# Windowed attention and a gated feed-forward: the gate's low part through PSUM, offsets for the first chunks, and the weights' checks placed by a count

## The chip, the cores and the metric

The kernel runs on one core of one Trainium2 chip. The metric is the device time of one execution in microseconds (us), taken as the median of several runs. TensorE (PE) multiplies matrices and writes to PSUM; VectorE (DVE), ScalarE (ACT) and GpSimd (POOL) work element by element, and POOL works on SBUF alone in this kernel; SyncE (SP) issues the DMAs. Each engine has one queue and runs it in order: an instruction that waits holds up everything behind it on its engine.

## The reference

Two layers, one after the other, in float32. The first is attention over 4 batches, 8 heads, 768 positions of 64 elements, where a position sees the 4 first positions (sinks) and the last 128. The second takes the attention's output as 3072 tokens of 512 elements.

```python
scores = q @ k.T / sqrt(64)                       # per batch and head
keep = (pos_k < 4) | ((0 <= rel) & (rel < 128))   # rel = pos_q - pos_k
a = softmax(where(keep, scores, -1e9))
x = (a @ v) as 3072 x 512
h = x @ w_in                                      # 512 x 2048
g = h * cos(h)
out = g @ w_out                                   # 2048 x 512
```

## The kernel before

**High and low parts.** Matrix products run in a rounded float32 format (fp32r). To keep precision, each operand is held as a rounded high part and a low part, the rest: `hi = round(a)`, `lo = a - hi`. A product is three matmuls, hi by hi, lo by hi and hi by lo. ACT makes the high part by a copy, and DVE or POOL the low part by a subtraction.

**Tiling.** The tokens are cut into 12 chunks of 256. Chunks 0, 1 and 2 are the first 256 positions of batches 0, 1 and 2; their 24 heads are "early": their scores and values are plain float32 matmuls (L737, L925), and the x of their chunks is split by a trick on PE. `x_minus` (L327) adds to the values in PSUM the product of minus the identity and the high part, so that the low part is left there to be copied out (L370, L372). Minus the identity lies in the tile `minus`, which is the first half of `gt`, a buffer that is used later for the sinks.

Each chunk has 8 slots; a slot is 256 of the 2048 hidden columns. There are 96 slots, numbered m = 8a + s for chunk a and slot s. A slot goes through these steps:

- `h_mm` (L381): 24 matmuls of 128 x 256 into a bank of PSUM, the h bank. Chunks 0 and 1 turn over two banks (b4, b2), later ones over three (b4, b2, b3).
- `turns` (L390, ACT) and `rest` (L396, DVE): h in whole turns, and the fraction r that is left of it, in SBUF.
- `cosine` (L403, ACT): r becomes the cosine, by a table of sines. A softmax on ACT needs the table of exponentials, so a change of tables lies between.
- `gate` (L408, DVE): h in PSUM times the cosine, written over r in SBUF. With it the h bank is free.
- `g_hi` (L414, ACT) and `g_lo` (L420, DVE or POOL): the gate's high and low part.
- `out_mm` (L429): 12 matmuls of 128 x 512 into two accumulators, banks b0 and b1. After 8 slots they are copied out (L370, L372) into the tiles `raw` and stored.

**Attention, head by head.** SP loads q, k, v; q and k are turned (L713 by PE for early heads, L695 and L766 by DVE for the others) and split (L778, L784); PE makes scores (L737, L793), DVE masks them (L806), ACT takes the exponential (L815). For four or two heads together DVE makes the denominators (L824, L825), after which every head's p is normalised on POOL, DVE or ACT (L835), transposed by PE (L895), split (L904, L911) or copied, and multiplied by v (L949). The sinks' columns go by a way of their own (L867, L877).

**Weights.** Where the weights come as 64-bit pairs (the case here), 32 pieces of 128 x 512 pairs are loaded into two `raw` tiles and converted. Each piece is loaded once more later, to be checked: `check_piece` has SP load the piece and DVE reduce it to one number per partition (L533), in the column of `tiny`. At the end one number of all of `tiny` decides whether a general path must run again. A check takes a turn of the two `raw` tiles, which the accumulators' copies use too. From chunk 2 on, a slot has one check until all 32 are placed.

**What sets the order.** Nothing reorders the code at run time. The class `Plan` collects every step with the engines that could do it, their durations as estimates, the steps and buffers that it waits for, and a priority: the slot's time t, plus a constant of the step's kind from the table `C`. It then goes through time with a list of ready steps for each engine and always takes the one with the lowest priority; where several engines could do it, by further constants. `emit` writes the steps out in that order. So the constants move each step in the engines' queues, and a changed step moves those around it.

## Time and profile before

| | us |
|---|---|
| runs | 771.24, 774.18, 778.17 |
| median | 774.18 |
| profiled execution, its own time | 773.9 |
| its span | 772.1 |
| mean granted TensorE clock | 0.993 |
| PE busy | 748.2 (97%) |
| weight loads of PE busy | 660.9 (86%) |
| DVE busy | 608.5 (79%) |
| ACT busy | 577.9 (75%) |
| POOL busy | 150.5 (19%) |

The span is the time from the first to the last recorded instruction; the execution's own time holds a little more, 1.8 us here. The engine with the most work is PE. Of its chain of waits, "PE h L381" holds 31% and "PE acc L429" 29% of the span. A share over the whole span hides the stages: the first 120 us, in which weights and the first heads arrive; the middle, in which attention of later chunks runs beside the slots of earlier ones; and the end, in which only slots are left. The views by stretches below keep them apart.

### The profile page before, as it was taken

Reading aid. Unit: us, or ns where it says so; the run is one execution under the profiler, and the core shown is the slowest. Engines: PE = TensorE matmul, PEld = TensorE weight load, DVE = VectorE, ACT = ScalarE, POOL = GpSimd, SP = SyncE. Lnnn points to the kernel's source line nnn. Section 1 sums busy time; section 2 is a strip of 40 time slices with the busy share of each in tenths; the row PEclk is TensorE's granted clock in tenths of the full one; section 3 lists DMA queues with packets and bytes.
Section 4 is the critical chain, followed back from the end, with each engine's and each line's share of the span. In section 5 each row is a group of like instructions: output and inputs, shape, how many; then the busy total and the mean of one; then the engine's idle time right before and its main releaser. Section 6 shows DMA issues by size and latency. Waiting matters only on the chain.

```text
span 772.1 us, 15308 instructions
## 1 busy us (share of the span) xinstructions
PE 748.2 (97%) x4987; PEld 660.9 (86%) x4987; DVE 608.5 (79%) x1597; ACT 577.9 (75%) x1345; POOL 150.5 (19%) x233
## 2 busy tenths in 40 slices
PE   7899999999989999999999999999999999999996
PEld 6566777888978989888899999999999999999995
DVE  6868888778868889989989988888878988964432
ACT  2779796878868787787787887897798788784332
POOL 2122210100313432212234321210211221220000
PEclk9999999999999999999999999999999999999998
DMA  5655464332455366275367243232242233110000
GB/s 149 173 158 170 133 192 156 65 57 39 88 157 110 56 185 163 40 191 138 65 164 187 45 114 54 46 70 45 38 87 53 46 76 60 31 39 1 28 1 32
DMA packets 215673, 71.50 MB, mean 93 GB/s; under 512 B 204320, under 2 KB 204320, under 8 KB 215584
## 3 DMA queue, kind: packets, MB, share of 16 engines
q1 hardware_dynamic: 215584, 70.43, 38.2%
q8 instruction: 41, 0.67, 0.4%
q14 instruction: 48, 0.39, 0.2%
HBM read 64.10 MB, written 6.29 MB: 91 GB/s over the span
## 4 chain that ended last, share of the span: by engine, by line
PE 80%; DVE 7%; DMA 5%; ACT 4%; issue 2%; SPq 1%; DVEq 0%; ACTq 0%
PE h L381 31%; PE acc L429 29%; PE av L949 5%; PE tp L895 4%; PE s L793 4%; DMA raw<-in_moe_w_in_dram 3%; PE s L737 2%; PE av L925 2%; DMA xk<-in_k_dram 1%; ACT p L815 1%; PE gp L877 1%; DVE p L806 1%; DVE plo L911 1%; DVE r L396 1%; SPq L675 1%
## 5 line engine op out<-in xcount | busy, mean ns | idle before, releaser
L381 PE MATMUL h<-xhi,whi_in 128*128 128x256 f32 x768 | 224.0, 292 | 2.4 <-DVE r L408 2.4
L381 PE MATMUL h<-xlo,whi_in 128*128 128x256 f32 x768 | 217.2, 283 | 0.1
L381 PE MATMUL h<-xhi,wlo_in 128*128 128x256 f32 x768 | 216.9, 282 | 0.0
L381 PEld LDWEIGHTS h<-xhi,whi_in 128*128 128x128 f32 x768 | 145.8, 190 | 15.3 <-issue 4.5
L429 PE MATMUL acc<-whi_out,ghi 128*128 128x512 f32 x384 | 157.5, 410 | 0.0
L381 PEld LDWEIGHTS h<-xhi,wlo_in 128*128 128x128 f32 x768 | 146.1, 190 | 7.5
L429 PE MATMUL acc<-wlo_out,ghi 128*128 128x512 f32 x384 | 151.7, 395 | 0.0
L429 PE MATMUL acc<-whi_out,glo 128*128 128x512 f32 x384 | 150.5, 392 | 0.0
L381 PEld LDWEIGHTS h<-xlo,whi_in 128*128 128x128 f32 x768 | 145.8, 190 | 0.3 <-DVE xlo L337 0.3
L806 DVE CUSTOM_DVE_ANT_0 p<-s,mk 128x264 f32<-128x264 f32 (+1 forms) x192 | 76.8, 400 | 33.2 <-PE s L793 21.8
L815 ACT ACTIVATE p<-p,st 128x264 f32<-128x264 f32 (+1 forms) x192 | 93.4, 489 | 0.7
L403 ACT ACTIVATE r<-r,neg 128x512 f32<-128x512 f32 x96 | 69.0, 723 | 26.7 <-DVE r L396 24.3
L429 PEld LDWEIGHTS acc<-whi_out,glo 128*128 128x128 f32 x384 | 72.2, 188 | 16.5
L420 DVE TENSOR_TENSOR glo<-r,ghi 128x512 fp32r<-128x512 f32 x82 | 57.7, 703 | 31.3 <-ACT ghi L414 30.5
L414 ACT CAST ghi<-r 128x512 fp32r<-128x512 f32 x96 | 59.0, 615 | 30.0 <-PE acc L429 29.0
L429 PEld LDWEIGHTS acc<-whi_out,ghi 128*128 128x128 f32 x384 | 72.6, 189 | 5.0 <-issue 0.7
L429 PEld LDWEIGHTS acc<-wlo_out,ghi 128*128 128x128 f32 x384 | 73.0, 190 | 3.8 <-DVE wlo_out L518 0.3
L408 DVE TENSOR_TENSOR r<-h,r 128x512 f32<-128x512 f32 x96 | 65.2, 680 | 11.7 <-ACT r L403 11.4
L390 ACT ACTIVATE yt<-h 128x512 int32<-128x512 f32 x96 | 57.1, 595 | 18.1 <-PE h L381 16.0
L396 DVE SCALAR_TENSOR_TENSOR r<-h,yt 128x512 f32<-128x512 f32 x96 | 65.6, 683 | 5.4 <-ACT yt L390 4.0
L835 POOL TENSOR_SCALAR p<-p,st 128x264 f32<-128x264 f32 (+2 forms) x65 | 36.7, 576 | 156.3 <-DVE st L825 122.3
L848 POOL TENSOR_TENSOR vr<-v,vr 128x192 fp32r<-128x192 f32 (+1 forms) x59 | 34.9, 591 | 160.6 <-ACT vr L843 143.2
(128 smaller groups left out, 1392.8 us busy)
## 6 DMA issues: line engine op xcount, KB each, us to landing
raw<-in_moe_w_in_dram SPq DMA_DIRECT2D x32, 512.0 KB
raw<-in_moe_w_out_dram SPq DMA_DIRECT2D x32, 512.0 KB
xk<-in_k_dram SPq DMA_DIRECT2D x256, 48.0 KB
out_dram<-raw SPq DMA_DIRECT2D x24, 256.0 KB
v<-in_v_dram SPq DMA_DIRECT2D x64, 96.0 KB
xq<-in_q_dram SPq DMA_DIRECT2D x144, 32.0 KB
v<-in_v_dram SPq DMA_DIRECT2D x32, 64.0 KB
xq<-in_q_dram SPq DMA_DIRECT2D x24, 64.0 KB
```

The source lines that it names most:

```text
L381: nc.tensor.matmul(out=o.h[:, t, :], lhsT=w[:, c, fs], rhs=xx[:, c, :], start=(c == 0 and n == 0), stop=(c == NC - 1 and n == 2),)
L390: nc.scalar.activation(out=yt, in_=o.h, func=AF.Copy, scale=INV2PI, bias=0.25)
L396: nc.vector.scalar_tensor_tensor(out=o.r, in0=o.h, scalar=INV2PI, in1=yt, op0=ALU.mult, op1=ALU.subtract)
L403: nc.scalar.activation(out=o.r, in_=o.r, func=AF.Sin, scale=TWOPI_DOWN, bias=quarter)
L408: nc.vector.tensor_tensor(out=o.r, in0=o.h, in1=o.r, op=ALU.mult)
L414: nc.scalar.copy(out=o.ghi, in_=o.r)
L420: e.tensor_tensor(out=o.glo, in0=o.r, in1=f32(o.ghi), op=ALU.subtract)
L429: nc.tensor.matmul(out=x.acc[j], lhsT=gg[:, t, j * P : (j + 1) * P], rhs=w[:, f, :], start=(f == 0 and n == 0), stop=(f == NFT - 1 and n = ...
L806: nc.vector.tensor_tensor_reduce(out=o.p[:, j, :w], in0=o.s_ps[j][:, :w], in1=masks[min(o.i0 + j, 2)][:, :w], op0=ALU.add, op1=ALU.min, sc ...
L815: nc.scalar.activation(out=o.p[:, j, :w], in_=o.p[:, j, :w], func=AF.Exp, bias=o.lead.st[:, 0, o.nth, j : j + 1], scale=-1.0, accum_out=o. ...
L835: e.tensor_scalar(out=o.p[:, j, :w], in0=o.p[:, j, :w], scalar1=r, scalar2=1.0, op0=ALU.mult, op1=ALU.mult)
L949: nc.tensor.matmul(out=dst, lhsT=lhs, rhs=rhs, start=(n == 0), stop=(n == len(seq) - 1), skip_group_check=True)
```

## The change

- `gate` writes its product back over h in PSUM. `g_hi` reads it there, and `g_lo` subtracts from it there; since POOL isn't given PSUM, `g_lo` runs on DVE alone. r is free after the gate, and the h bank only after the low part has been made.
- In chunks 0 and 1 there is a new way (`GM` is 2): `g_minus` adds minus the identity times the high part to the h bank on PE, one matmul of 128 x 512, and `g_rest` copies what is left out as the low part, on ACT or DVE.
- For this the start and stop marks of `h_mm` stand once for the bank rather than once for each half of it.
- The table `FIRST` gives each kind of step in chunks 0, 1 and 2 an offset of its own, and the weights' pieces a slope.
- The checks are placed so that those still missing are no more than 0.87 for each of the last eight slots and 0.371 for each slot before them.
- The constants of `C` are new.

```diff
+    "ALT": 0.104, "BLF": 0.065, "CK": 15.581, "CR": 0.87, "CS": 0.371, "DA": -3.061, "DH": -1.801, "DM": -0.625,
...
+    "POOLF": 0.622, "POOLPEN": 6.121, "PRE": 4.5, "R": 2, "RAW": 2, "SAME": 0.176, "SEM": 0.204, "SPE": 0.29,
...
+FIRST = {
+    "A": [16.64, 4.98, -6.05], "H": [0.49, 0.51, 5.97], "L": [-3.43, 4.39, -1.69], "M": [5.14, -1.3, 1.47],
...
+    def extra(kind, a):
+        return FIRST[kind][a] if a < 3 else 0.0
...
                     nc.tensor.matmul(
                         out=o.h[:, t, :], lhsT=w[:, c, fs], rhs=xx[:, c, :],
-                        start=(c == 0 and n == 0), stop=(c == NC - 1 and n == 2),
+                        start=(t == 0 and c == 0 and n == 0), stop=(t == FG - 1 and c == NC - 1 and n == 2), skip_group_check=True,
                     )
...
-            nc.vector.tensor_tensor(out=o.r, in0=o.h, in1=o.r, op=ALU.mult)
+            nc.vector.tensor_tensor(out=o.h, in0=o.h, in1=o.r, op=ALU.mult)
...
-            nc.scalar.copy(out=o.ghi, in_=o.r)
+            nc.scalar.copy(out=o.ghi, in_=o.h)
...
-            e.tensor_tensor(out=o.glo, in0=o.r, in1=f32(o.ghi), op=ALU.subtract)
+            e.tensor_tensor(out=o.glo, in0=o.h, in1=f32(o.ghi), op=ALU.subtract)
+        return fn
+
+    def g_minus(o):
+        def fn(e):
+            nc.tensor.matmul(out=o.h, lhsT=minus, rhs=o.ghi, start=False, stop=True, skip_group_check=True)
+        return fn
+
+    def g_rest(o):
+        def fn(e):
+            o.glo = mp.tile([P, FG, NT], F32R, name=f"glo_{o.m}", tag="glo", bufs=C["GLO"])
+            copy(e, o.glo, o.h)
         return fn
...
-            a6 = add(sub(FG * NT), g_lo(o), [a5, blo], t + C["DM"] + 10.8, port=True)
-            br.users += [a5, a6]
+            br.users.append(a4)
+            a5 = add([("ACT", act(FG * NT, False))], g_hi(o), [a4, bhi], tm + 10.2)
+            users = [a0, a2, a4, a5]
+            if plan.minus and a < C["GM"]:
+                m = add([("PE", 0.23)], g_minus(o), [a5], tm + 10.5)
+                bhi.users.append(m)
+                env.minus.users.append(m)
+                c = [("ACT", act(FG * NT, False)), ("DVE", dve(FG * NT))]
+                a6 = add(c, g_rest(o), [m, blo], tm + 10.8)
+                users.append(m)
+            else:
+                a6 = add([("DVE", dve(FG * NT))], g_lo(o), [a5, blo], tm + 10.8)
+            bh.users += users + [a6]
...
-            if a > 1 and len(checked) < len(checks):
+            left = len(slots) - nh
+            while len(checked) < len(checks) - C["CR"] * min(left, NSLOT) - C["CS"] * max(left - NSLOT, 0):
                 checked.append(check_piece(plan, t + C["CK"], len(checked), checks[len(checked)][2]))
```

The order of the steps that comes out, at three places. The rows are instructions as they stand in one engine's queue: line, operation, output, inputs, shape. The number after `h_`, `r_` or `glo_` is the slot; after `p_` or `st_` come batch, block of positions and head. In the changed kernel the lines lie 11 to 32 further down.

PE's queue in chunk 0 before the change, between the last accumulating matmul of slot 0 and the first h of slot 4, which takes the bank of slot 2:

```order
L429 MATMUL acc_0_1_912<-whi_out_91,glo_0_836 128x512
L713 MATMUL qk_2_0_2_954<-ident_79,xq_74 128x128 x2
L713 MATMUL qk_2_0_2_954<-ident_79,xk_75 128x128 x2
L895 MATMUL tp_1_0_4_970<-ident_79,p_1_0_4_672 128x128 x3
L381 MATMUL h_4_984<-xhi_0_405,whi_in_89 128x256
```

And now, with the new matmul for slot 2 (L436) ahead of the h of slot 4:

```order
L770 MATMUL s_2_0_3_1_1056<-tk_2_0_2_984,tq_2_0_2_977 128x256
L436 MATMUL h_2_854<-ghi_2_1046,gt_80 128x512
L928 MATMUL tp_1_0_7_1065<-ident_79,p_1_0_7_814 128x128 x3
L338 MATMUL av_1_0_6_1049<-xhi_1_760,gt_80 64x256
L392 MATMUL h_4_1076<-xhi_0_413,whi_in_89 128x256
```

Before, the bank of slot 2 was free when its gate had run; now four short matmuls stand between the minus and the h that takes the bank over, and the copy of the low part has to run beside them.

DVE's queue in chunk 2 before, where the second of two checks stands ahead of a softmax's denominators and normalisations:

```order
L533 ISA wt1_73,tiny_87<-raw1_71 128x512
L533 ISA tiny_87 128x1
L824 TENSOR_SCALAR st_0_2_4_1987<-st_0_2_4_1987 128x8
L825 RECIPROCAL st_0_2_4_1987<-st_0_2_4_1987 128x8
L835 TENSOR_SCALAR p_0_2_4_1986<-p_0_2_4_1986,st_0_2_4_1987 128x264 x2
L835 TENSOR_SCALAR p_0_2_5_2150<-p_0_2_5_2150,st_0_2_4_1987 128x264
L408 TENSOR_TENSOR r_20_2554<-h_20_2467,r_20_2554 128x512
```

And a place in chunk 4 now, one of five of this kind:

```order
L555 ISA wt1_73,tiny_87<-raw1_71 128x512
L555 ISA tiny_87 128x1
L857 TENSOR_SCALAR st_1_2_4_3761<-st_1_2_4_3761 128x8
L858 RECIPROCAL st_1_2_4_3761<-st_1_2_4_3761 128x8
L799 STREAM_TRANSPOSE tk_1_4_2_4297<-xk_75 128x3x128
L419 TENSOR_TENSOR h_35_4126<-h_35_4126,r_35_4208 128x512
L407 SCALAR_TENSOR_TENSOR r_36_4318<-h_36_4217,yt_81 128x512
L898 CAST gc_186<-p_1_2_4_3760 128x2x8
```

The checks stand ahead of the denominators at both; the normalisations have left DVE's queue, for POOL's and ACT's. Over the whole kernel DVE has 75 of the 192 normalisations before and none after, POOL 65 and 133, ACT 52 and 59.

DVE's queue in the last chunk before:

```order
L396 SCALAR_TENSOR_TENSOR r_92_9818<-h_92_9756,yt_81 128x512
L408 TENSOR_TENSOR r_92_9818<-h_92_9756,r_92_9818 128x512
L420 TENSOR_TENSOR glo_91_9859<-r_91_9771,ghi_91_9849 128x512
L396 SCALAR_TENSOR_TENSOR r_93_9864<-h_93_9805,yt_81 128x512
L408 TENSOR_TENSOR r_93_9864<-h_93_9805,r_93_9864 128x512
```

And now:

```order
L555 ISA wt0_72,tiny_87<-raw0_70 128x512
L555 ISA tiny_87 128x1
L431 TENSOR_TENSOR glo_91_9859<-h_91_9718,ghi_91_9852 128x512
L407 SCALAR_TENSOR_TENSOR r_93_9879<-h_93_9821,yt_81 128x512
L555 ISA wt1_73,tiny_87<-raw1_71 128x512
```

Seven checks have moved here, and the low part reads the h bank. Of the other checks, about three stand in each chunk from the third to the eleventh. The low part of chunks 0 and 1 is a copy, eleven times on ACT and five times on DVE, and POOL, which made fourteen low parts before, makes none.

More of the change, by code (lines that the diff above doesn't have):

```diff
@@ L54, in __init__ @@
         self.steps, self.bufs, self.port, self.ahead = [], {}, set(), set()
+        self.minus = False
     def buf(self, tag, n):
@@ L562, in dense @@
                     mm.append(
-                        add([("PE", 0.655)], h_mm(o, x, tt, half), d + mm[-1:], t + C["DH"] + (3.5, 5.8)[tt] + 0.6 * half)
+                        add([("PE", 0.655)], h_mm(o, x, tt, half), d + mm[-1:], t + C["DH"] + extra("H", a) + (3.5, 5.8)[tt] + 0.6 * half)
                     )
@@ L566, in dense @@
             x.blo.users += mm
-            a0 = add([("ACT", act(FG * NT, False))], turns(o), mm + [by], t + C["DM"] + 7.2)
-            a2 = add([("DVE", dve(FG * NT))], rest(o), [a0, br], t + C["DM"] + 8.0)
+            tm = t + C["DM"] + extra("M", a)
+            a0 = add([("ACT", act(FG * NT, False))], turns(o), mm + [by], tm + 7.2)
+            a2 = add([("DVE", dve(FG * NT))], rest(o), [a0, br], tm + 8.0)
             by.users.append(a2)
-            a3 = add([("ACT", act(FG * NT) + 0.09)], cosine(o), [a2], t + C["DM"] + 8.9, table="sin")
-            a4 = add([("DVE", dve(FG * NT))], gate(o), [a3], t + C["DM"] + 9.5)
-            bh.users += [a0, a2, a4]
-            a5 = add([("ACT", act(FG * NT))], g_hi(o), [a4, bhi], t + C["DM"] + 10.2)
-            a6 = add(sub(FG * NT), g_lo(o), [a5, blo], t + C["DM"] + 10.8, port=True)
-            br.users += [a5, a6]
+            a3 = add([("ACT", act(FG * NT) + 0.09)], cosine(o), [a2], tm + 8.9, table="sin")
+            a4 = add([("DVE", dve(FG * NT))], gate(o), [a3], tm + 9.5)
+            br.users.append(a4)
[11 more added lines that the diff above has]
+            bh.users += users + [a6]
             for tt in range(FG):
@@ L603, in banded_path @@
         plan = Plan()
+        plan.minus = True
         add, buf = plan.add, plan.buf
@@ L1052, in before_softmax @@
                     oo.bl = buf("l", C["L"])
-                    q1 = add([("ACT", act(NT))], q_hi(o, oo), [q0, oo.bl], t - 6 * T + C["DQ"] + 0.6)
-                    oo.ql = add([("DVE", dve(NT))], q_lo(o, oo), [q1], t - 6 * T + C["DQ"] + 0.9, port=True)
+                    q1 = add([("ACT", act(NT))], q_hi(o, oo), [q0, oo.bl], t - 6 * T + dq + 0.6)
+                    oo.ql = add([("DVE", dve(NT))], q_lo(o, oo), [q1], t - 6 * T + dq + 0.9, port=True)
                     btq.users += [q1, oo.ql]
@@ L1142, in after_softmax @@
             bav = buf("av", 1)
-            p0 = add([("PE", 0.107 * o.n)], turn(o), o.nm + [pt], t + C["DA"] + 1.3)
+            p0 = add([("PE", 0.107 * o.n)], turn(o), o.nm + [pt], t + da + 1.3)
             o.bp.users.append(p0)
-            p1 = add([("ACT", act(o.n * P, False))], p_hi(o), [p0, bhi], t + C["DA"] + 1.8)
-            p2 = add([("DVE", dve(o.n * P))], p_lo(o), [p1, blo], t + C["DA"] + 2.3)
+            p1 = add([("ACT", act(o.n * P, False))], p_hi(o), [p0, bhi], t + da + 1.8)
+            p2 = add([("DVE", dve(o.n * P))], p_lo(o), [p1, blo], t + da + 2.3)
             pt.users += [p1, p2]
@@ L1158, in after_softmax @@
             bxb = buf("xb", 1)
-            y1 = add([("ACT", act(NT, False))], x_low(o), [y0, bxb], t + C["DA"] + 4.8)
+            y1 = add([("ACT", act(NT, False))], x_low(o), [y0, bxb], t + da + 4.8)
             if o.odd == 0:
                 x.bf = buf("x", 1)
-            y2 = add([("DVE", dve(NT))], x_sum(o, x), [y0, y1] + (x.sums[o.pair] or [x.bf]), t + C["DA"] + 5.1)
+            y2 = add([("DVE", dve(NT))], x_sum(o, x), [y0, y1] + (x.sums[o.pair] or [x.bf]), t + da + 5.1)
             bav.users += [y1, y2]
```

80 lines of the change are left out of this document (41 added, 39 removed).

## The prediction

> **What bounds the kernel now.** I read the busy time of each engine by stretches first, to see which engine is full where. The columns are the stretch, its length, the busy time of TensorE (PE), of its weight loads, of VectorE (DVE), ScalarE (ACT) and GpSimd (POOL) with the number of instructions, the granted TensorE clock, the DMA share and GB/s.
>
> ```profile
> 0.00:20.00 20.00, 15.39 (x79) 13.21 (x79) 11.81 (x48) 5.05 (x12) 4.03 (x13) 0.91 0.54 148
> 20.00:120.00 100.00, 93.24 (x530) 67.09 (x530) 81.67 (x216) 81.71 (x214) 19.89 (x22) 1.00 0.59 166
> 120.00:200.00 80.00, 80.00 (x504) 68.31 (x505) 62.63 (x156) 60.59 (x130) 6.84 (x12) 1.00 0.32 73
> 200.00:250.00 50.00, 47.32 (x321) 43.02 (x319) 38.15 (x102) 39.47 (x93) 13.03 (x16) 0.97 0.52 127
> 250.00:450.00 200.00, 197.31 (x1397) 180.41 (x1396) 180.23 (x482) 160.59 (x379) 60.13 (x90) 1.00 0.51 121
> 450.00:650.00 200.00, 200.00 (x1416) 184.78 (x1415) 171.09 (x463) 167.59 (x392) 37.13 (x66) 1.00 0.32 63
> 650.00:750.00 100.00, 100.00 (x680) 91.69 (x679) 58.33 (x130) 58.00 (x125) 9.48 (x14) 1.00 0.09 23
> 750.00:772.10 22.10, 14.98 (x74) 12.33 (x73) 4.58 (x8) 4.88 (x8) 0.00 (x0) 0.91 0.08 28
> ```
>
> PE is never idle in 120 to 200 and in 450 to 750. What another engine saves there is worth nothing; what is added to PE there is paid in full. PE idles 100 - 93.24 = 6.8 us in 20 to 120, 50 - 47.32 = 2.7 us in 200 to 250 and 200 - 197.31 = 2.7 us in 250 to 450. A change can win only there, at the first 20 us, or at the end.
>
> Then the waits by pairs of engines (us in total, times, longest), and the timeline at those that PE takes part in:
>
> ```profile
> DVE wt L533 <- DMA raw<-in_moe_w_in_dram: 5.8, 4, 2.4
> PE tp L895 <- DVE p L835: 2.1, 1, 2.1
> ...
> 218.56 0.69 DVE L533 CUSTOM_DVE_ANT_0 wt<-raw 128x512 f32<-128x512 f32 x1 [2.35 <-DMA raw<-in_moe_w_in_dram]
> 220.08 0.69 DVE L533 CUSTOM_DVE_ANT_0 wt<-raw 128x512 f32<-128x512 f32 x1 [0.83 <-DMA raw<-in_moe_w_in_dram]
> 220.70 0.17 DVE L824 TENSOR_SCALAR st<-st 128x8 f32<-128x8 f32 x1
> 221.65 1.10 PE L895 MATMUL tp<-ident,p 128*128 128x128 f32 x4 [2.14 <-DVE p L835]
> 282.97 0.38 PE L877 MATMUL gp<-ident,gc 128*48 128x128 f32 x2 [0.18 <-DVE gc L867]
> 344.31 0.38 PE L877 MATMUL gp<-ident,gc 128*48 128x128 f32 x2 [1.13 <-DVE gc L867]
> ```
>
> Here the checks of the weights (L533) show. Two of them stand in DVE's queue ahead of the softmax's denominators (L824). DVE stands still 2.35 and 0.83 us for their loads, the denominators come late, the normalised scores (L835) come late, and PE waits 2.14 us at its transposes. The wait costs more than itself, since the clock falls behind it:
>
> ```profile
> 221.50:222.50 1.00, 0.85 (x5) 0.65 (x5) 1.00 (x3) 1.00 (x4) 0.85 (x2) 0.66 0.77 307
> 222.50:223.50 1.00, 1.00 (x7) 1.00 (x6) 1.00 (x6) 0.96 (x2) 0.00 (x0) 0.50 0.82 258
> 223.50:224.50 1.00, 1.00 (x7) 1.00 (x7) 1.00 (x2) 0.44 (x1) 0.00 (x0) 0.50 0.42 160
> 224.50:225.50 1.00, 1.00 (x7) 0.95 (x7) 0.52 (x3) 0.16 (x1) 0.00 (x0) 0.64 0.12 49
> ```
>
> The lost clock is 0.34 + 0.50 + 0.50 + 0.36 = 1.7 us of PE's time. In a sentence beside it: the Trainium skill, "TensorE: Matmul & The Clock Gate", section "What's actually happening", lets the clock fall after an idle window of about 3.4 us; by this rule a wait of 2.14 us alone costs no clock, the 1.7 us would not come back with it, and the sum below would be 773.3. The row, where the clock was 0.50 right behind that wait, decides for 771.6.
>
> **The change part by part.** Durations of the work that moves, by groups (busy us, mean ns; then idle before, by releaser), two accumulating matmuls from the timeline, and three steps of the chain that ended last:
>
> ```profile
> L420 DVE TENSOR_TENSOR glo<-r,ghi 128x512 fp32r<-128x512 f32 x82 | 57.7, 703 | 31.3 <-ACT ghi L414 30.5
> L414 ACT CAST ghi<-r 128x512 fp32r<-128x512 f32 x96 | 59.0, 615 | 30.0 <-PE acc L429 29.0
> L904 ACT CAST phi<-tp 128x512 fp32r<-128x512 f32 x64 | 37.4, 584 | 3.8 <-PE tp L895 2.1
> L835 DVE TENSOR_SCALAR p<-p,st 128x264 f32<-128x264 f32 x53 | 20.8, 448 | 0.4
> L835 POOL TENSOR_SCALAR p<-p,st 128x264 f32<-128x264 f32 x49 | 27.9, 582 | 89.6 <-DVE st L825 77.7 <-ACT ghi L414 7.7 <-PE acc L429 4.3
> L372 DVE COPY pt<-tp 128x384 f32<-128x384 f32 x3 | 1.7, 555 | 1.5 <-PE tp L895 1.5
> L815 ACT ACTIVATE p<-p,st 128x264 f32<-128x264 f32 x128 | 64.8, 508 | 0.5
> L815 ACT ACT_TABLE_LOAD x26 | 33.4, 1283 | 0.4
> L327 PE MATMUL av<-xhi,gt 64*64 64x256 f32 (+1 forms) x24 | 7.6, 320 | 1.1 <-ACT xhi L319 0.6 <-ACT xlo L370 0.5
> ...
> 706.64 0.40 PE L429 MATMUL acc<-whi_out,ghi 128*128 128x512 f32 x1
> 706.87 0.40 PE L429 MATMUL acc<-wlo_out,ghi 128*128 128x512 f32 x1
> ...
> 672.25 1.43 PE acc L429 x6
> 747.62 1.43 PE h L381 x12
> 753.97 10.92 PE acc L429 x48
> ```
>
> 1. Sixteen matmuls by minus the identity are new on PE, 128 x 512 each. Accumulating matmuls of that width start 0.23 us apart (706.64 to 706.87): 16 x 0.23 = 3.7 us, in stretches where PE is busy 93 to 100%. **+3.7.**
>
> 2. PE waits at them, and at the next use of their bank. The nearest row is the same trick that the kernel has for x (L327, 24 times): 1.1 us of idle, for 16 of them 0.7 us. That is the lower end. Above: chunks 0 and 1 turn over two banks, and the bank is now free only when the minus has ended (0.40) and its copy has run (0.58, the row of L904): 0.98 us. The order of slots 2 to 5 leaves a few short matmuls between the minus and the next h of that bank, about 0.7 us: 4 x 0.3 = 1.2 us. Without that cover it is 4 x 0.98 = 3.9. I take **+1.2**, as the order shows the cover.
>
> 3. The checks, 32 before and after, become fewer while attention runs: one a slot in chunks 2 to 5 before, about three a chunk after, seven in the last three slots. Idle in 200 to 450 goes, with the lost clock: 2.7 + 1.7 + 2.7 = 7.1. **-7.1.** This is the most that the checks can give, since I put every wait in that stretch down to them; the least is nothing.
>
> 4. Some of it comes back. In five later chunks the order has two checks in a row right ahead of the denominators, as at 218.56. If each cost what that place cost (2.14 + 1.7) it would be 19 us; if DVE's queue has slack, nothing. The other two places where PE waits behind checks' work cost 0.18 and 1.13, a mean of 0.65. I take that, since those, like the five, have PE work in flight ahead: 5 x 0.65 = **+3.3**.
>
> 5. In 20 to 120 DVE loses nine subtractions of the low part (9 x 0.70 = 6.3) and some ten normalisations (10 x 0.45 = 4.5), and takes about six copies of transposed scores (6 x 0.56 = 3.4): -7.4, of 81.7 busy. ACT takes eleven copies of the low part (11 x 0.58 = 6.4) and loses six others (3.4): +3.0, also of 81.7. Offsets bring loads and attention forward for some chunks and back for others. PE idles 6.8 us there; the gain lies between that and a loss of ACT's 3.0. One engine relieved, another loaded, I take half: **-3.4.**
>
> 6. All 75 normalisations that DVE did go to POOL or ACT, about 75 x 0.4 = 30 us, and the subtractions of the low part on POOL go to DVE. POOL's norm is 0.58 against DVE's 0.45; it idled 89.6 us before these. PE was full in 450 to 750: nothing is won. Beside POOL a check could also take longer:
>
> ```profile
> 242.53 1.07 POOL L784 TENSOR_TENSOR r<-tk,r 128x408 fp32r<-128x408 f32 x1 [3.83 <-ACT r L778]
> 242.70 1.44 DVE L533 CUSTOM_DVE_ANT_0 wt<-raw 128x512 f32<-128x512 f32 x1 [1.78 <-DMA raw<-in_moe_w_in_dram]
> ```
>
> 1.44 against 0.69 at 218.56: 0.75 us more beside a POOL operation of 1.07. The added POOL work is some 68 x 0.58 = 39 us; at 0.7 us for each of them DVE would take 27 us longer in all, about what its 30 us of norms leave. DVE idles 200 - 171 = 29 us in 450 to 650 besides. **0** for DVE as a whole; where a stretched check stands ahead of the denominators it is a rival, below.
>
> 7. In the last chunk seven checks of 0.69 us join 58 us of DVE work in 100. The last 48 accumulating matmuls (10.92 us at the end of the chain) and the store behind stay. **0**, to +1.
>
> Sum against the profiled run, 773.9 us (span 772.1; 0.3 under the median of 774.18): 773.9 + 3.7 + 1.2 - 7.1 + 3.3 - 3.4 = **771.6**. A measurement of this kernel tells about 1% from no change, 766.4 to 781.9, so this is "within 1%".
>
> **The rivals.** *Faster, 764.* The front's idle goes whole, no check comes back to PE, the minus waits at its lower end: 773.9 + 3.7 + 0.7 - 7.1 - 6.8 = 764.4. For it speaks that DVE and ACT, both busy 82%, are what PE waits for there; against it, that ACT gets more. Lower still: a matmul takes 93.24 / 530 = 0.176 us in 20 to 120 and 80 / 504 = 0.159 in 120 to 200, 9 us over 530, which a better order could halve: 760.
>
> *Same, 779: the checks still cost.* 25 of the 32 stand among attention's work yet, so idle of the same size could return there, and the front stays: 773.9 + 3.7 + 1.2 = 778.8. The change would then not do what it moves the checks for. POOL's new norms lead to the same time in another way: if both checks at the five places were stretched by 0.75, as at 242.70, 5 x 2 x 0.75 = 7.5 us is added to 771.6: 779.1. For it speaks that row; against it, that the check before it, at 220.08, was not stretched, and that POOL's norms follow the denominators, which follow the checks. In a sentence beside it: the Trainium skill, "SBUF — State Buffer", section "Who interferes with whom", has a VectorE instruction with two SBUF inputs, as the check is, contend with GpSimd reading SBUF; the trace agrees with its 1.44 against 0.69.
>
> *Slower, 786: the h bank is held too long.* Before, the gate wrote to SBUF and freed the bank. Now the high part (0.62) and the low part (0.70) must read it too. Behind the last matmul that frees the high part's buffer, the order leaves as little as 12 h and 6 accumulating matmuls before the next h of that bank: 1.43 + 1.43 = 2.9 us. Spare: 2.9 - 1.32 = 1.5 us. A softmax that stands first on ACT is eight exponentials of 0.51 and a table load of 1.28, 5.4 us, far over the spare. If that happens twice a chunk in ten chunks and PE waits 0.7 each, it is 14 us: 771.6 + 14 = 786. It passes the 1% from 10.3 / 20 = 0.5 us each. Against it: the shortest place is in the last chunk, where no softmax runs; elsewhere attention's matmuls stand between too. The five checks at their full price (19 instead of 3.3: 787) end in the same place.
>
> **How the numbers follow.** Forecast 0.34, the two ways to 779 together 0.16, faster 0.34, slower 0.16. So within 1% has 0.50. The forecast's own range is 766 to 776. To hold 8 in 10 the range goes down to 759, past the faster case, and up to 783, into the slower one, leaving about 0.07 below and 0.12 above.
>
> **What would show it.** Right: in the stretch 200 to 450 PE idles under 2 us and the clock stays at 1.00; idle before the minus under 1.5 us in all; PE's idle before h on "DVE glo" or "ACT glo" near nothing from chunk 2 on; in 20 to 120 PE busy about 96 to 97. Wrong: PE waiting at h for a low part, transposes waiting for L835's successor on POOL behind checks (2 us with a clock of 0.50 behind it), or a front as idle as before. The prediction falls if PE's own work grows by more than the 16 matmuls, or if the end after the last h is longer than 10.92 us plus its store.

## The result

The changed kernel takes 782.85 us (median of 20 runs, 777.62 to 791.26), the kernel before 776.05 us (20 runs, 771.24 to 781.28). The ratio is 1.0085, with a 95% interval of 1.0063 to 1.0106: slower by 0.85%, less than the 1% that the prediction called "within 1%", but clearly on the other side of the forecast of 771.6 us.

The profiled execution of the changed kernel took 781.19 us (span 779.4). The busy time of each engine by stretches, as shown of before:

```profile
0.00:20.00 20.00, 15.41 (x81) 13.41 (x81) 11.41 (x49) 4.95 (x12) 2.61 (x12) 0.91 0.55 151
20.00:120.00 100.00, 92.07 (x476) 62.56 (x476) 75.32 (x200) 74.25 (x200) 19.57 (x27) 0.95 0.54 151
120.00:200.00 80.00, 79.54 (x480) 66.31 (x479) 57.01 (x136) 59.50 (x125) 9.05 (x19) 1.00 0.35 84
200.00:250.00 50.00, 50.00 (x361) 46.15 (x360) 39.11 (x102) 40.32 (x98) 14.71 (x24) 1.00 0.36 74
250.00:450.00 200.00, 199.67 (x1422) 183.69 (x1422) 163.80 (x441) 163.32 (x380) 57.72 (x101) 1.00 0.39 81
450.00:650.00 200.00, 198.48 (x1393) 182.09 (x1392) 159.80 (x428) 166.91 (x391) 55.19 (x98) 1.00 0.40 89
650.00:750.00 100.00, 100.00 (x687) 91.24 (x686) 65.07 (x152) 61.88 (x134) 13.89 (x26) 1.00 0.25 70
750.00:779.40 29.40, 21.40 (x117) 18.09 (x115) 9.39 (x20) 6.91 (x12) 0.00 (x0) 0.91 0.18 59
```

From 200 to 450 PE is full and at full clock: the idle of before is gone. From 20 to 120 it looks almost as busy as before (92.1 against 93.2 us), but it runs 476 matmuls where it ran 530, and its clock is 0.95. Busy time hides a slow clock, so the number of instructions has to be read with it.

To see where time is lost, I give each kind of matmul (same operands and shape) a pace, the value under which a third of its start-to-start times in the trace of before lie. What a matmul's start-to-start time exceeds that is counted as lost in the stretch where it falls; it holds waits, half clock and late weight loads alike. The sum of the paces is PE's own work. The first 1.7 us, in which PE has hardly begun, are left out. In us:

| | PE's own work | lost 0–76 | 76–120 | 120–200 | 200–450 | 450 to PE's end | after PE's end |
|---|---|---|---|---|---|---|---|
| before | 714.5 | 17.0 | 6.5 | 4.0 | 15.4 | 5.9 | 7.1 |
| changed | 718.2 | 17.7 | 13.0 | 5.0 | 6.8 | 9.0 | 8.0 |
| difference | +3.7 | +0.7 | +6.5 | +1.0 | -8.6 | +3.1 | +0.9 |

The differences make 7.3 us, that of the spans (779.4 - 772.1). So the middle gains more than was forecast, and the front loses it again. Each profile is one execution, and how long the clock stays low differs between executions of one kernel (last section), so a loss in the front is known to some 2 to 3 us.

**The front.** The place is at 79 to 85 us. First the waits of PE in the timeline, then ACT's timeline up to the instruction that PE waits for, each of the changed kernel:

```profile
79.77 0.84 PE L928 MATMUL tp<-ident,p 128*128 128x128 f32 x3 [0.60 <-ACT p L866]
81.11 0.70 PE L770 MATMUL s<-tk,tq 64*128 64x256 f32 x2 [0.50 <-DVE st L839]
84.83 0.77 PE L770 MATMUL s<-tk,tq 64*128 64x128 f32 x2 [1.76 <-ACT tk L381]
```

```profile
79.31 1.79 ACT L866 ACTIVATE p<-p,st 128x128 f32<-128x128 f32 x5 [0.23 <-DVE st L858]
81.01 0.57 ACT L401 ACTIVATE yt<-h 128x512 int32<-128x512 f32 x1
81.48 0.50 ACT L866 ACTIVATE p<-p,st 128x256 f32<-128x256 f32 x1
81.99 1.28 ACT L414 ACT_TABLE_LOAD   x1
83.28 0.72 ACT L414 ACTIVATE r<-r,neg 128x512 f32<-128x512 f32 x1
83.91 0.60 ACT L537 CAST whi_out<-wt 128x512 fp32r<-128x512 f32 x1
84.42 0.36 ACT L381 COPY tk<-qk 128x256 f32<-128x256 f32 x1
```

ACT normalises six blocks, turns h, changes its table, takes a cosine and converts a weight, and only then copies the turned k for which the scores wait. PE has no h and no accumulating matmuls to put in between. Behind the waits the clock falls (stretches of the changed kernel; the last number but two is the clock):

```profile
84.00:86.00 2.00, 1.17 (x4) 0.77 (x4) 1.97 (x6) 2.00 (x6) 0.00 (x0) 0.72 0.86 239
86.00:88.00 2.00, 2.00 (x7) 0.92 (x5) 1.26 (x4) 0.04 (x1) 0.00 (x0) 0.50 0.25 69
...
92.00:94.00 2.00, 2.00 (x7) 1.51 (x6) 1.05 (x2) 0.00 (x0) 0.00 (x0) 0.50 0.00 0
94.00:96.00 2.00, 2.00 (x8) 1.26 (x8) 0.78 (x4) 0.62 (x2) 0.00 (x0) 0.72 0.85 256
```

It is 0.50 in the four stretches from 86 to 94: 2 x 0.28 + 4 x 2 x 0.50 + 2 x 0.28 = 5.1 us lost, beside the 2.9 us of waits. The half clock is thus most of what the front loses: without it 76 to 120 has 13.0 - 5.1 = 7.9 us, against 6.5 before, where the clock was 1.00.

**After 450 us** PE waits again behind checks, at a place of the kind that the order had shown. DVE's, POOL's and PE's timeline of the changed kernel:

```profile
461.84 0.69 DVE L555 CUSTOM_DVE_ANT_0 wt<-raw 128x512 f32<-128x512 f32 x1 [0.96 <-DMA raw<-in_moe_w_in_dram]
463.67 0.69 DVE L555 CUSTOM_DVE_ANT_0 wt<-raw 128x512 f32<-128x512 f32 x1 [1.12 <-DMA raw<-in_moe_w_in_dram]
464.28 0.17 DVE L857 TENSOR_SCALAR st<-st 128x8 f32<-128x8 f32 x1
464.86 1.41 POOL L868 TENSOR_SCALAR p<-p,st 128x264 f32<-128x264 f32 x3 [10.27 <-DVE st L858]
465.40 0.79 PE L928 MATMUL tp<-ident,p 128*128 128x128 f32 x3 [0.96 <-POOL p L868]
```

Two checks wait for their loads, the denominators (L857) stand behind them, POOL's normalisation behind these, and PE's transposes wait 0.96 us.

### The profile page after: what moved, and what is told of

Read it like the earlier page. It is cut to its first block, busy times and chain, and to the rows that moved or that the text cites. A ratio compares the mean times of both kernels' runs of the same rounds, so it can differ in the third digit from the quotient of the medians.

```text
span 779.4 us, 15305 instructions
## 1 busy us (share of the span) xinstructions
PE 756.6 (97%) x5003; PEld 663.5 (85%) x5003; DVE 580.9 (75%) x1522; ACT 578.0 (74%) x1347; POOL 172.8 (22%) x306
## 5 line engine op out<-in xcount | busy, mean ns | idle before, releaser
L451 PE MATMUL acc<-whi_out,ghi 128*128 128x512 f32 x384 | 155.9, 406 | 0.0
L868 POOL TENSOR_SCALAR p<-p,st 128x264 f32<-128x264 f32 (+2 forms) x133 | 62.3, 491 | 161.6 <-DVE st L858 129.4
L451 PEld LDWEIGHTS acc<-whi_out,glo 128*128 128x128 f32 x384 | 72.5, 189 | 16.6
L419 DVE TENSOR_TENSOR h<-h,r 128x512 f32<-128x512 f32 x96 | 66.0, 693 | 27.7 <-ACT r L414 27.5
L414 ACT ACTIVATE r<-r,neg 128x512 f32<-128x512 f32 x96 | 69.2, 724 | 15.9 <-DVE r L407 15.4
L881 POOL TENSOR_TENSOR vr<-v,vr 128x192 fp32r<-128x192 f32 (+1 forms) x62 | 37.0, 597 | 172.3 <-ACT vr L876 148.1
L425 ACT CAST ghi<-h 128x512 fp32r<-128x512 f32 x96 | 55.8, 581 | 19.1 <-PE acc L451 17.2
L431 DVE TENSOR_TENSOR glo<-h,ghi 128x512 fp32r<-128x512 f32 x80 | 54.7, 684 | 15.3 <-ACT ghi L425 15.0
```

What stands on the lines that cost most here:

```text
L414: nc.scalar.activation(out=o.r, in_=o.r, func=AF.Sin, scale=TWOPI_DOWN, bias=quarter)
L419: nc.vector.tensor_tensor(out=o.h, in0=o.h, in1=o.r, op=ALU.mult)
L425: nc.scalar.copy(out=o.ghi, in_=o.h)
L431: e.tensor_tensor(out=o.glo, in0=o.h, in1=f32(o.ghi), op=ALU.subtract)
L451: nc.tensor.matmul(out=x.acc[j], lhsT=gg[:, t, j * P : (j + 1) * P], rhs=w[:, f, :], start=(f == 0 and n == 0), stop=(f == NFT - 1 and n = ...
L868: e.tensor_scalar(out=o.p[:, j, :w], in0=o.p[:, j, :w], scalar1=r, scalar2=1.0, op0=ALU.mult, op1=ALU.mult)
```

## The experiments

All ratios are to the kernel before, from runs side by side. The table at the end of this section splits each profile as above.

**Parts of the changed kernel taken away, order kept.**

`e1`, the sixteen matmuls by minus the identity, so that this kernel leaves out the low part of the gate in chunks 0 and 1:

```diff
     def g_minus(o):
         def fn(e):
-            nc.tensor.matmul(out=o.h, lhsT=minus, rhs=o.ghi, start=False, stop=True, skip_group_check=True)
+            pass
```

> The changed kernel, every queue in the same order, without the sixteen matmuls by minus the identity (the low part of the gate in chunks 0 and 1 is left out; the copies that would fetch it stay). Theory: they cost PE their own time alone, 16 x 0.23 = 3.7 us, so the time is about 779 against 783 for the changed kernel (1.004 of before instead of 1.0085), and the wait of PE near 84 us with the half clock behind it stays. Rival: the bank that is held for them, and their order on PE, make the slow front; then 8 us or more go, about 775, and the wait near 84 us is gone too.

777.91 us, ratio 1.0032 (0.9998 to 1.0065), against 1.0085: 0.53% or 4.1 us less, with an uncertainty of some 3 us. That agrees with the matmuls' own time, 3.7 us. In its profile the wait of 1.76 us is still there, at 88.20 us, with half clock for 3.4 us behind it, and the front still loses 9.8 us in 76 to 120. The theory holds. The rival's time, 775, lies at the edge of the interval, but its other sign, that the wait goes, did not come.

`e2`, two copies moved ahead, in ACT's and in DVE's queue:

```diff
...
+        steps.insert(place(cosines[2], "ACT"), steps.pop(place(early[2, 0, 2].k0, "ACT")))
+        steps.insert(place(rests[3], "DVE") + 1, steps.pop(place(early[2, 0, 2].q0, "DVE")))
```

> The changed kernel with two steps moved: ACT's copy of the turned k of batch 2, head 2 goes ahead of the change of tables for slot 2's cosine, and DVE's copy of the turned q of the same head ahead of one step of a weight's conversion. Theory: PE's wait of 1.76 us near 84 us goes, and with it the half clock that holds to 95 us (some 5 us): 776 to 778. If only the wait goes and the clock falls all the same, 781. Rival: the front is slow for all of its work together, and PE waits for the next step instead: 783 as before.

780.51 us in four runs, ratio 1.0103 (1.0052 to 1.0153): no gain that these runs show. In its profile the wait of 1.76 us is gone, as the theory said, and what is lost in 76 to 120 falls from 13.0 to 9.9 us. The clock falls all the same, behind two waits of 0.5 us (timeline and stretches of this kernel):

```profile
80.35 0.84 PE L931 MATMUL tp<-ident,p 128*128 128x128 f32 x3 [0.52 <-ACT p L869]
81.69 0.70 PE L773 MATMUL s<-tk,tq 64*128 64x256 f32 x2 [0.50 <-DMA raw<-in_moe_w_out_dram]
```

```profile
82.00:84.00 2.00, 2.00 (x7) 0.96 (x6) 1.91 (x5) 1.98 (x4) 0.30 (x1) 0.59 0.00 0
84.00:86.00 2.00, 1.97 (x7) 1.05 (x6) 1.76 (x5) 1.99 (x6) 0.00 (x0) 0.50 0.44 111
86.00:88.00 2.00, 2.00 (x7) 1.05 (x6) 2.00 (x6) 0.64 (x2) 0.00 (x0) 0.50 0.76 230
88.00:90.00 2.00, 2.00 (x6) 1.02 (x6) 0.10 (x1) 1.23 (x3) 1.05 (x1) 0.70 0.80 267
```

So one late copy is not the front's cause. That it is a part of 3 us is not shown either, since `e1`, with the copy as late as ever, lost 9.8 us: less the half clock (5.1 us in the changed kernel, 1.7 in `e1`, 3.4 here) the stretch loses 7.9, 8.1 and 6.5 us, which leaves to the copy about 1.5 us, its wait.

`e7`, POOL's normalisations after 120 us on DVE:

```diff
-            for _, _, fn, e in steps:
+            for t, _, fn, e in steps:
+                if e == "POOL" and t > 120 and fn.__qualname__.endswith("norm.<locals>.fn"):
+                    e = "DVE"
                 fn(engines[e])
```

> The changed kernel, every queue in the same order, but with POOL's normalisations after the first 120 us on DVE at the same place in time. Theory: PE's waits of 0.3 to 1.9 us for a normalised p from POOL (at 347, 465, 583 and 641 us) are what was given back after 450 us; they go, and 2 to 3 us with them: 780. Rival: DVE, with some 45 us more work, is late for masks and gates, and PE waits for these: 783 or more.

791.35 us, ratio 1.022 (1.0177 to 1.0262): the rival. The wait at the same place is now longer, for a p from DVE (timeline of this kernel):

```profile
468.15 0.69 DVE L555 CUSTOM_DVE_ANT_0 wt<-raw 128x512 f32<-128x512 f32 x1 [2.28 <-DMA raw<-in_moe_w_in_dram]
469.62 0.44 PE L930 MATMUL tp<-ident,p 128*128 128x128 f32 x2 [1.53 <-DVE p L870]
```

So POOL was not what made it late: the check and its load are, one step further up. After 120 us, in this order, having the normalisations off DVE is worth 1.022 against 1.0085.

**The checks in the kernel before.**

`e3`, without them, order kept, so that their loads go as well as their work on DVE:

```diff
...
-        i = add(dma(1), lambda e: e.dma_start(out=raw.rearrange("p n w -> p (n w)"), in_=src), [r], prio - 6, lat=2.6)
+        i = add(dma(1), lambda e: None, [r], prio - 6, lat=2.6)
...
         def least(e):
-            nc.vector.tensor_tensor_reduce(
+            pass
```

> The kernel before, every queue in the same order, without the 32 checks of the weights (their loads and their work on DVE are left out; nothing is checked). Theory: the idle of PE between 200 and 450 us is the checks' doing, so that 7 to 8 us go: 767 to 769, PE without a wait over 0.6 us there, the clock at 1.00 throughout. Rival: half of that idle has other causes (the sinks' columns, scores waiting for masks): 771 to 773.

767.7 us, ratio 0.9906 (0.9879 to 0.9932): 7.2 us, as forecast. The stretches of this kernel show where:

```profile
200.00:250.00 50.00, 50.00 (x351) 46.09 (x351) 38.17 (x99) 44.10 (x102) 14.59 (x19) 1.00 0.30 59
250.00:450.00 200.00, 199.69 (x1425) 184.37 (x1425) 168.70 (x442) 164.50 (x385) 59.02 (x91) 1.00 0.32 60
```

The idle of 2.7 us in each of the two stretches was the checks' doing, and so was the lost clock. Whether it was their place in DVE's queue or the traffic of their loads, this run does not part; the timeline at 218.56 us speaks for the queue.

`e4`, the changed kernel's rule for the checks, and only that:

```diff
+    "ALT": 2.669, "BLF": -0.052, "CK": 15.581, "CR": 0.87, "CS": 0.371, "DA": -3.097, "DH": -2.747, "DM": -0.791, "DQ": 10.525, "DS": -2.397,
...
-            if a > 1 and len(checked) < len(checks):
+            left = len(slots) - nh
+            while len(checked) < len(checks) - C["CR"] * min(left, NSLOT) - C["CS"] * max(left - NSLOT, 0):
```

> The kernel before with the changed kernel's rule for the checks alone (32 checks, placed by the count, and their own constant). Up to about 195 us its order is that of the kernel before. Theory: the gain of the changed kernel in 200 to 400 us (8 us) comes from the checks' placing: 767 to 770, faster than both. Rival: it comes from the norms that left DVE or from the new constants: 774 to 777, with waits behind checks as before.

771.69 us, ratio 0.9982 (0.9961 to 1.0002). In its profile 200 to 450 loses 7.9 us instead of 15.4, and what follows loses 7.9 instead of 5.9. The theory holds for the middle; over the whole, a gain is not shown.

`e13`, the same with 0.45 in place of 0.371, so that no check stands ahead of slot 35 (in its profile the first runs at 331 us).

> The kernel before with the changed kernel's way of placing the checks and 0.45 in place of 0.371 a slot, so that the first check comes at slot 35 and none in 200 to 300 us. Theory: the wait near 220 us goes entirely and the few checks of each later chunk cost little: 769 to 771 (0.992 to 0.996 of before), faster than both kernels. Rival: each check among attention costs what it costs, wherever it stands: 772 to 774, no different from 0.371.

775.48 us, ratio 1.002 (0.9983 to 1.0057): nothing gained, and no better than the rival had it. Its profile loses 15.3 us after 450, with a wait like the one at 221.65 us of before (timeline of this kernel):

```profile
629.85 0.69 DVE L533 CUSTOM_DVE_ANT_0 wt<-raw 128x512 f32<-128x512 f32 x1 [2.85 <-DMA raw<-in_moe_w_out_dram]
631.07 0.16 DVE L824 TENSOR_SCALAR st<-st 128x8 f32<-128x8 f32 x1
632.01 0.74 PE L895 MATMUL tp<-ident,p 128*128 128x128 f32 x3 [1.85 <-DVE p L835]
```

`e8` (`"CK": 15.581, "CR": 2.0, "CS": 2.0`) has two checks a slot in the last sixteen slots.

> The kernel before with its 32 checks in the last 16 slots, two a slot, where DVE is busy 58 us in 100. Theory: all the idle that checks make goes, as without checks: 766 to 769 (0.989 to 0.993 of before), faster than with the changed kernel's rule (771.7). Rival: the loads, 32 in 90 us, and the two raw tiles that the accumulators' copies need as well, hold up the copies and the last stores: 771 to 775.

786.15 us, ratio 1.0167 (1.0118 to 1.0216): the rival, and slower than it. Up to 650 us this kernel loses no more than the one without checks; of the 25.8 us in its last column but one, 21 are lost after that. DVE's timeline at the end, and what PE waited for:

```profile
771.21 0.69 DVE L533 CUSTOM_DVE_ANT_0 wt<-raw 128x512 f32<-128x512 f32 x1 [4.71 <-DMA raw<-in_moe_w_out_dram]
773.69 0.69 DVE L533 CUSTOM_DVE_ANT_0 wt<-raw 128x512 f32<-128x512 f32 x1 [1.78 <-DMA raw<-in_moe_w_out_dram]
774.66 0.37 PE L1247 MATMUL tp<-ident,tmin 128*1 128x128 f32 x1 [13.44 <-DVE tmin L1245]
```

The loads, not DVE's work, set the pace of the checks, and the last of them end after everything else.

`e11` (`"CK": 12.0, "CR": 1.5, "CS": 1.5`, and counted as if the kernel ended four slots earlier) keeps them off the very end.

> The kernel before with its 32 checks from slot 71 to slot 92, three in two slots, so that the last have their loads before the end. Theory: the 23 us lost after 650 us with two a slot to the last slot came from loads behind which DVE's low parts and the last check stood; here most of it goes, and the 10 us that that kernel was ahead at 650 us stay in part: 766 to 770. Rival: two raw tiles let through one check in 3 us or more, DVE still stands ahead of the low parts, and PE waits in the last 100 us: 773 or more.

774.7 us, ratio 0.9981 (0.9946 to 1.0015): the rival, by its time. Of the 25.8 us of `e8` half are gone, but with 12.3 us after 450, against 5.9 before, what 200 to 450 gains (5.8 us lost there) goes in good part.

**The new gate and the new constants, each alone.**

`e9` has the new gate and the minus, with the constants `C` and the checks of before and zeros in `FIRST`.

> The new gate in PSUM and the sixteen matmuls by minus the identity, with the constants and the rule for the checks of the kernel before and no offsets. Theory: the slow front is the new constants' and offsets' doing; here the accumulating matmuls of slot 0 start before 80 us, the checks cost their 7 us as before, and only the matmuls and a us or two of waits for their bank are added: 778 to 780. Rival: the bank that is held in chunks 0 and 1 makes the front slow by itself: h of slot 4 after 92 us, 783 or more.

780.75 us, ratio 1.0058 (1.0025 to 1.0092), 4.5 us: near the theory. h of slot 4 starts at 85.3 us (82.8 before, 98.8 changed), slot 0 accumulates from 71.7 us (73.9, 88.0).

`e10` is the changed kernel with the gate of before:

```diff
-            nc.vector.tensor_tensor(out=o.h, in0=o.h, in1=o.r, op=ALU.mult)
+            nc.vector.tensor_tensor(out=o.r, in0=o.h, in1=o.r, op=ALU.mult)
...
-            nc.scalar.copy(out=o.ghi, in_=o.h)
+            nc.scalar.copy(out=o.ghi, in_=o.r)
...
-            e.tensor_tensor(out=o.glo, in0=o.h, in1=f32(o.ghi), op=ALU.subtract)
+            e.tensor_tensor(out=o.glo, in0=o.r, in1=f32(o.ghi), op=ALU.subtract)
...
+            bh.users += [a0, a2, a4]
+            a5 = add([("ACT", act(FG * NT))], g_hi(o), [a4, bhi], tm + 10.2)
+            a6 = add(sub(FG * NT), g_lo(o), [a5, blo], tm + 10.8, port=True)
+            br.users += [a5, a6]
```

> The gate of the kernel before (in SBUF, its bank free after it, the low part on DVE or POOL, no minus) in all chunks, with the constants, the offsets and the rule for the checks of the changed kernel. Theory: the front stays slow, with the accumulating matmuls of slot 0 after 85 us, and the middle stays fast: 776 to 779, as with the gate of two chunks in SBUF (778.2). Rival: the gate in PSUM is what costs, also later on; then 768 to 772.

779.85 us, ratio 1.0058 (1.002 to 1.0095): near the theory again. Slot 0 accumulates from 89.0 us. So each half of the change costs about 0.6% by itself, and the late start of slot 0's accumulating matmuls belongs to the constants and offsets. The front's loss does not fall to one half alone: 76 to 120 loses 7.2 us with the new gate alone and 9.1 with the constants alone, 6.5 before and 13.0 in the changed kernel, and 1.7 of the 9.1 and 5.1 of the 13.0 are half clock.

`e5` gives back the old gate in chunks 0 and 1 alone, the edit of `e10` under `if own`, with `own = o.own = plan.minus and a < 2`, the low part on DVE alone, and `"GM": 0`.

> The changed kernel with the gate of chunks 0 and 1 in SBUF as before: no minus, the low part a subtraction on DVE, the h bank free after the gate. Everything else is the changed kernel's, and the plan orders it anew. Theory: in the front two banks are held until the low part is made, the low part waits for a high part's buffer, that for the accumulating matmuls of slot 0, and those for w_out; so h of slot 4 starts at 99 us instead of 83 and PE has nothing dense to run in 79 to 98. Without it h of slot 4 starts before 90 us, the clock stays up, and 3.7 + 5 us go: 774 (0.998 to 1.001 of before). Rival: the offsets of the first chunks make the front slow; then only the 16 matmuls' 4 us go: 778 to 779, as without the minus alone, and the clock still falls near 84 us.

778.19 us, ratio 1.0069 (1.0018 to 1.012). h of slot 4 does start earlier, at 90.7 us, but 76 to 120 loses 13.6 us, as much as with the minus: the loss has moved to 100 to 120 us. Only the matmuls' time is gained, as the rival had it. The bank held for the low part delays h; that it makes the front slow, this profile does not show.

`e6` sets every offset in `FIRST` to zero.

> The changed kernel with all offsets of the first chunks at zero; the plan orders it anew. Rival theory (the offsets): the accumulating matmuls of slot 0 start near 75 us again instead of 88, and 5 us or more go: 774 to 778. Theory (the bank): h of slot 4 starts after 92 us all the same and the front stays slow: 781 to 786.

799.35 us, ratio 1.0322 (1.0265 to 1.0378). Neither theory had this: the offsets do not cause the front's loss, they hold it down. Under the new `C` without them 0 to 120 loses 39.1 us.

`e12` has w_out's weights earlier, `"WO": 3.0` for 7.981.

> The changed kernel with one constant changed, the weights' time for w_out (8.0 to 3.0, before it was 7.3 beside other slots' times): its first piece is converted as the 12th of all, as in the kernel before, not as the 14th, and the plan orders all anew. Theory: the front is slow in 76 to 100 us because the accumulating matmuls of slot 0 have no w_out until 88 us and PE has nothing dense to run between late normalisations; here they start before 80 us, PE has more than 64 records in 80 to 100, the clock stays up, and 4 to 6 us go: 777 to 779. Rival: VectorE's and ScalarE's work for the attention of chunks 1 and 2 is what is late in any order; then the loss only moves to 100 to 130 us: 781 to 785.

785.57 us, ratio 1.0137 (1.0101 to 1.0174): the rival, and a little slower than it. Slot 0 accumulates from 79.7 us, 80 to 100 has 115 records at full clock, and 100 to 120 pays for it (stretches of this kernel):

```profile
80.00:100.00 20.00, 20.00 (x115) 14.74 (x114) 16.75 (x41) 16.89 (x38) 1.97 (x5) 1.00 0.49 153
100.00:120.00 20.00, 17.49 (x81) 12.85 (x81) 14.84 (x36) 11.44 (x30) 4.93 (x8) 0.86 0.47 138
```

`e14` and `e15` exchange the eleven constants by which the plan picks an engine (ALT, BLF, NM, NW, NWF, PEN, POOLF, POOLPEN, SAME, SEM, SPE): the old ones in the changed kernel, the new ones in the kernel before.

> The changed kernel with the eleven constants by which the plan picks an engine for a step set back to those before (of the 192 normalisations DVE takes a good part again, POOL fewer); times, offsets, gate and checks stay. Theory A, the choice of engines makes the front and the give-back after 450 us: the normalisations that left DVE for POOL and ACT come later to PE; with the old choice 4 to 6 us come back, 777 to 779. Theory B, the times of the steps make it: 782 to 786, and PE still has fewer than 90 records in 80 to 100 us or loses as much up to 140.

783.97 us, ratio 1.0091 (1.0052 to 1.0129): theory B, no gain. In its profile the loss lies earlier, at 40 to 80 us, with the clock at 0.50 from 63 to 80 us.

> The kernel before with those eleven constants of the changed kernel, so that no normalisation is on DVE (150 of 192 on POOL), and nothing else changed. Theory A: the front slows and PE waits for normalised p from POOL throughout: 779 to 783. Theory B: the choice is worth little either way, 773 to 777, with the checks' waits between 200 and 450 as before.

786.75 us, ratio 1.0161 (1.0095 to 1.0226), slower than either theory had it: in the kernel before, the new choice costs 1.6% by itself, against 0.85% for the whole change. Why is not known. The profiled execution, at 813.51 us, had a clock of 0.50 from 8 to 83 us and again from 131 to 144 us; the other four took 786.33 to 791.11 us and left no trace.

The profiles split as before, in us. Part of the first column is not the edits' doing. In `e3`, `e5`, `e6`, `e10`, `e12` and `e14` the clock was 0.50 for 10 to 14 us from about 8 to 10 us on, where it was 0.50 for 3.4 us before and in the changed kernel, and in `e1` it fell at 31 and at 55 us instead; that makes some 2 to 4 us. Up to there `e3` and `e1` have the order of the kernel that they were made from (`e3` sets `tiny` on POOL besides), so that in them, at least, it is most likely the chance of one execution. `e15` is left out.

| | PE's own work | lost 0–76 | 76–120 | 120–200 | 200–450 | 450 to PE's end | after it |
|---|---|---|---|---|---|---|---|
| e1 no minus | 714.5 | 21.6 | 9.8 | 5.6 | 7.6 | 7.1 | 7.6 |
| e2 turn first | 718.2 | 18.3 | 9.9 | 4.8 | 7.9 | 9.3 | 7.7 |
| e7 norms on DVE | 718.2 | 17.5 | 13.2 | 5.0 | 10.4 | 14.1 | 7.5 |
| e3 before, no checks | 714.5 | 20.7 | 5.1 | 6.9 | 6.5 | 5.9 | 7.2 |
| e4 before, new checks | 714.5 | 16.9 | 6.5 | 4.0 | 7.9 | 7.9 | 8.4 |
| e13 before, even checks | 714.5 | 16.3 | 6.5 | 4.0 | 6.5 | 15.3 | 7.6 |
| e8 before, late checks | 714.5 | 16.7 | 6.5 | 4.0 | 5.8 | 25.8 | 8.2 |
| e11 before, checks to slot 92 | 714.5 | 17.0 | 6.6 | 4.0 | 5.8 | 12.3 | 7.7 |
| e9 new gate alone | 718.2 | 16.6 | 7.2 | 5.0 | 12.4 | 7.2 | 7.7 |
| e10 old gate | 714.5 | 19.4 | 9.1 | 5.6 | 9.6 | 10.3 | 7.6 |
| e5 gate in SBUF | 714.5 | 19.7 | 13.6 | 3.6 | 7.5 | 8.7 | 7.7 |
| e6 no offsets | 718.2 | 25.6 | 13.5 | 7.3 | 10.1 | 10.1 | 7.6 |
| e12 w_out earlier | 718.2 | 20.3 | 8.6 | 9.7 | 6.7 | 10.5 | 7.6 |
| e14 old choice | 718.2 | 24.1 | 8.2 | 4.7 | 8.7 | 10.2 | 7.8 |

None of these does the whole work and is shown to be faster than the kernel before.

## Why the prediction was wrong

1. *The sixteen matmuls, +3.7.* Right: PE's own work grew by 3.7 us, and without them the ratio fell by 0.53%, 4.1 us.

2. *Waits at the minus, +1.2.* Too high, but small: 0.3 us at the minus, and nothing at an h that takes its bank. The group of the new matmul (changed kernel), with all waits of PE for its high part:

```profile
L436 PE MATMUL h<-ghi,gt 128*128 128x512 f32 x16 | 7.4, 461 | 0.3 <-ACT ghi L425 0.3
```

3. *The checks, -7.1.* Right as the price of the checks (7.2 us without them), and the changed kernel's middle gained 8.6.

4. *Some of it comes back, +3.3.* The size is right, 3.1 us more lost after 450, but partly by luck: PE's waits for a normalised p come to 1.3 us there, 0.96 at 465.40 behind two checks and 0.35 at 641.00, and the rest is spread in pieces with no wait. The clock did not fall there, as the 19 us at the far end supposed. That moving the checks is worth little in the sum, -7.1 + 3.3, was not taken far enough: alone it gives 0.9982 and 1.002, no difference that is shown.

5. *The front, -3.4, between -6.8 and +3.0.* This step failed. 0 to 200 us lost 0.7 + 6.5 + 1.0 = 8.2 us more, of which 5.1 are the half clock from 84 to 96. It went wrong in two ways. The step counted how much DVE and ACT had to do, found it less on one and more on the other, and took half of PE's idle as a gain. It did not ask when PE would have dense work: slot 0 accumulates 14 us later, at 88.0 us, and its matmuls no longer fill the waits at 79 to 85 us. (That this alone makes the front slow is not shown; `e12` brought them to 79.7 us and lost as much behind them.) Nor did it let a wait cost clock in the front, though it had priced just that at 221.65 us. With +8.2 in its place, and without the 1.2 of step 2, which lies in the same stretch, the sum would have been 782.0; the profiled execution took 781.19.

6. *Normalisations off DVE, 0.* In the changed kernel no loss is seen from POOL's side: a check took 707 ns on average, 790 before. So the rival of checks stretched beside POOL did not come true; in DVE's group of the changed kernel they wait for loads. That the choice of engines is free is not shown, though: in the kernel before it cost 1.6% by itself (`e15`). The group:

```profile
L555 DVE CUSTOM_DVE_ANT_0 wt<-raw 128x512 f32<-128x512 f32 x32 | 22.6, 707 | 17.9 <-DMA raw<-in_moe_w_out_dram 11.1 <-DMA raw<-in_moe_w_in_dram 6.6
```

7. *The end, 0 to +1.* +0.9 in this profile; but the kernel before with other checks had 7.6 to 8.4 there, so that it is no more than these profiles differ by.

The slower rival had the right sign and the wrong mechanism. It priced the h bank, held until the low part is made, at 14 us after the front. PE lost next to nothing at h: before the 768 high-by-high matmuls, with which each slot's h begins, the changed kernel's page gives 0.7 us of idle, 2.4 before, and none of it behind a low part. Where the bank did delay h, in slot 4, freeing it moved the loss and won only the sixteen matmuls' time.

Of the signs named ahead, three came: PE idle 0.33 us in 200 to 450 at a clock of 1.00, 0.3 us of idle before the minus, and none at h behind a low part. The fourth did not: PE was to be busy 96 to 97 us in 20 to 120, and was 92.07. That the time stayed within 1% of before, as was forecast at even chances, is partly luck: the forecast had it 0.3% faster, by a gain in the front that was a loss.

What stays open is which of the constants makes the front slow. No part of the change does it alone: not the minus (`e1`), not the bank (`e5`, `e10`), not the offsets (`e6`), not w_out's time (`e12`), not the choice of engines (`e14`), though that choice does harm in the other order (`e15`). Each of `e5`, `e12` and `e14` mended the place at 80 us and lost as much elsewhere before 140. That the attention of chunks 1 and 2 on DVE and ACT is what is late in any such order fits all three, but was not tested by itself.

## What to carry to other kernels

Where a change moves a stage's work around, don't take the idle of the bound engine as the most that can be won and a little as the most that can be lost: look in the order for when dense work becomes ready, because without it short waits show, and they can cost more than their length again in clock (1.7 us behind 2.14, 5.1 behind 2.86, 3.4 behind 1.02). Work that is added to a full engine can be priced by its pace: 3.7 us by the traces, 4.1 by the runs, which tell it to some 3 us. Checks that wait for their own loads did harm where the instruction behind them in the queue feeds the bound engine; spread out or moved late they did it elsewhere, and only the kernel without them (0.9906) showed a gain.
